# Block-sparse attention and an MLP mixer on one Trainium2 core: queries and keys loaded two tokens to a partition

## Chip, cores and metric

The kernel runs on one core of a Trainium2 chip. The metric is the device time of one execution in microseconds (us); less is better. Engines are called PE (TensorE), DVE (VectorE), ACT (ScalarE), POOL (GpSimd) and SP (SyncE), as in the profile. PEld is PE's loading of stationary operands.

## What is computed

Inputs are q, k and v of shape (4, 8, 768, 64) and four weight matrices, all float32. Each of the 32 heads does block-sparse causal attention: the keys form 12 blocks of 64, each query scores the mean key of each block up to its own, and it attends to the three best blocks and to its own.

```python
k_rep = k.reshape(B, H, n_blocks, block, D).mean(axis=3)
gate_scores = np.einsum('bhsd,bhnd->bhsn', q, k_rep)
causal = pos[:, None] // block >= np.arange(n_blocks)[None, :]
gate_scores = np.where(causal, gate_scores, -1000000000.0)
top_idx = np.argsort(gate_scores, axis=-1)[..., -top_k:]
...
scores = scale * np.matmul(q, k.transpose(0, 1, 3, 2))
mask = mask & (pos[:, None] >= pos[None, :])
scores = np.where(mask, scores, -1000000000.0)
...
return np.matmul(attn, v).astype(np.float32)
```

The heads of a batch side by side make x (768 tokens, 512 channels), which goes through an MLP over tokens (768 to 256 to 768) with a residual sum u, and an MLP over channels (512 to 1536 to 512) with another:

```python
h = np.maximum(xt @ w_tok1, 0.0) @ w_tok2
u = x + h.transpose(0, 2, 1)
h2 = np.maximum(u @ w_ch1, 0.0) @ w_ch2
return (u + h2).astype(np.float32)
```

## The kernel before

The work is cut into 16 head pairs (two heads of one batch each). For a pair, `prepare` does this:

- `load_qk` (L312) loads k and then q into `kl` and `ql`, one token to a partition and six tokens to a row, with one DMA for each head (L319). Each piece that a DMA moves is one head's 64 values of a token, 256 bytes.
- `transposes` (L358) turns six 128x128 tiles on PE, in float32. Both heads' channels become the 128 partitions, the 768 tokens the columns. `evac_t` (L367) copies that from PSUM to `kt` or `qt` on ACT.
- `cast` (L376) on POOL writes each head's 64 rows as float16 into `KA` and `QA`, the operands of the score matmuls. Pair 0 is cast on ACT (L383).
- `ksum` (L388) sums the keys of each block on DVE, and `kcopy` (L396) puts the sums of both heads into `ks2` with two small reductions.
- The gate: `gate_q` (pair 0), `gate`, `gate_s`, `gate_r` (pairs 1 to 5) or `gate_t`, `gate_e`, `gate_b` (groups of two and of four pairs) multiply q with the block sums and bring the result to queries on partitions. Tokens 0 to 127 need no gate: they have at most two blocks. So five tiles of 128 queries remain (`GJ`).
- On DVE, `gm` (L465) adds the causal bias, `top` (L482) takes the eight largest of each 12 with one MAX8 per head and tile (L489, ten to a pair), `below` (L492) compares with the third, and `bias` (L503) makes 0 or -30000 of it.
- `mask` (L513) turns the result on PE into PSUM, float16, 24 rows to a pair. `put_mask` (L522) copies it on DVE to rows 64 to 87 of `QA`, once per head (L525). The same rows of `KA` hold an indicator of each key's block, so that the score matmul of 88 rows adds the mask by itself.

The pairs are prepared in the groups [0], [1], [2], [3], [4], [5], [6, 7], [8 to 11] and [12 to 15]. Gate and mask are made for a whole group, the mask copies of a group follow one another (two to a pair).

`attend` then makes, for each head, three groups of score matmuls (`scores`, L529), their exponentials on ACT (`expo`, L547), the causal product on the diagonal blocks on DVE (`diag`, L555, line L559), the product with v (`av`, L563, line L571, two heads one after the other in one PSUM bank) and the normalization on DVE (`recip`, `norm`, L579 and L590). Tiles of five pairs (`R`) stand in a ring: the casts of pair i wait for the scores of pair i - 5.

The mixer of a batch runs as soon as its four pairs are there, and its matmuls stand between those of later pairs: token mixing in L602 and L614 (batch 0: L633 and L647), the sums u in L622 and L656, the channel MLP in L683 (ch1), its relu on ACT (L693) and DVE (L695), L704 (ch2) and the last sum in L712. Three PSUM banks (`bank`) serve gate, mask and mixer; two double banks (`big`) serve transposes and scores. v comes with a cast on POOL's DMA queue (L326), the weights too (L732 to L737); q, k and the outputs are on SP's.

The order in which each engine gets its instructions is fixed when the program is built. `plan` (L157) is given every operation with its engine, its cost in ns, its dependencies, its priority and the buffers that it takes. It goes through them in time, by these costs, and lists them; the engines then execute in that order. Costs stand in `prepare` and `attend` (a mask copy 410, a pair's MAX8 720, a load `size=1750`). Where PE has nothing to do before 46 us by this list, matmuls on zeros (`dummy`, L719, line L721) are put in, 122 of them. `VAFTER` says after which cast each load of v is issued.

Of the kernel before, what the change touches and what calls it, by code (L numbers as in the profile page):

```python
# [39 lines left out]
def QACT(i):  # L40
# [3 lines left out]
VAFTER = [("kt", 1), ("kt", 2), ("qt", 2), ("qt", 3), ("qt", 3), ("qt", 4), ("qt", 6), ("qt", 8),  # L44
          ("qt", 11), ("qt", 12), ("qt", 13), ("qt", 14), ("kt", 15), ("qt", 15), ("qt", 15), ("qt", 15)]
DIRECT = (0,)
WSIZE = (2400, 4500)
GATE = {1: 400, 2: 1000, 3: 1000, 4: 1000}
# [174 lines left out]
def kernel(  # L223
# [23 lines left out]
    GJ = NJ - 1  # L247
# [25 lines left out]
    ks2 = [sp.tile([128, 32], FP, tag=f"ks{r}", name=f"ks{r}") for r in range(R)]  # L273
    bn16 = [sp.tile([128, GJ, 128], F16, tag=f"bn{y}", name=f"bn{y}") for y in range(NBN)]
# [4 lines left out]
    own4 = sp.tile([128, 4 * GJ, 2 * NB], FP, tag="own4", name="own4")  # L279
    gbias = sp.tile([128, GJ, 2 * NB], FP, tag="gbias", name="gbias")  # L280
    gown = sp.tile([128, 3 * GJ * NB], FP, tag="gown", name="gown")
    gone = gown[:, 0:GJ * NB].rearrange("p (j n) -> p j n", n=NB)
    own = gown[:, GJ * NB:].rearrange("p (j c) -> p j c", c=2 * NB)
# [5 lines left out]
    gt = sp.tile([128, S - 128], FP, tag="gt", name="gt")  # L289
# [22 lines left out]
    def load_qk(i, t32, src):  # L312
        b, h = pairs[i]

        def f():
            t = sb(t32, [128, NJ, 2 * D], FP, f"{t32}_{i}")
            T[t32, i] = t
            for g in range(2):
                nc.sync.dma_start(out=t[:, :, D * g:D * g + D], in_=src[b, h + g].rearrange("(j p) d -> p j d", p=128))  # L319
        return f  # L320
# [13 lines left out]
    def twice(t):  # L334
        return t.rearrange("p j (x n) -> p j x n", x=1).broadcast_to([128, GJ, 2, NB])

# [8 lines left out]

    def own_four():
        for c in range(4):
            nc.gpsimd.tensor_copy(out=own4[:, c:4 * GJ:4, :], in_=own)
        nc.gpsimd.tensor_copy(out=gbias.rearrange("p j (x n) -> p j x n", n=NB), in_=twice(gone))
# [8 lines left out]
    def transposes(t32, i):  # L358
        def f():
            p = ps("big", None, f"t{t32}")  # L360
            T["tr", t32, i] = p
            t = T[t32, i]
            for j in range(NJ):
                nc.tensor.transpose(out=p[:, 128 * j:128 * j + 128], in_=t[:, j, :], identity=ident32)  # L364
        return f
# [10 lines left out]
    def cast(dst, name, i, x):  # L376
        def f():
            lo = 64 * x
            to, src = dst[i % R][x][0:64, :], T[name, i][lo:lo + 64, :]
            nc.gpsimd.tensor_copy(out=to, in_=src)  # L380
        return f

    def cast_act(dst, name, i, x):  # L383
        def f():
            nc.scalar.copy(out=dst[i % R][x][0:64, :], in_=T[name, i][64 * x:64 * x + 64, :])
        return f

    def ksum(i):  # L388
        def f():
            kst = sp.tile([128, NB], FP, tag="kst", bufs=2, name=f"kst_{i}")  # L390
            T["kst", i] = kst
            kt = T["kt", i]
            nc.vector.tensor_reduce(out=kst, in_=kt.rearrange("p (n w) -> p n w", w=64), axis=AX.X, op=ALU.add)  # L393
        return f

    def kcopy(i):  # L396
        def f():
            kst = T["kst", i]
            r = i % R
            for lo, c in ((0, 0), (64, NB)):  # L400
                nc.vector.tensor_reduce(out=ks2[r][lo:lo + 64, c:c + NB],
                                        in_=kst[lo:lo + 64, :].rearrange("p (n o) -> p n o", o=1),
                                        axis=AX.X, op=ALU.add)
        return f

    def gate_q(i):
        def f():
            g = ps("bank", [128, 512], "gps")
            T["gps", i] = g[:, 0:2 * NB * GJ].rearrange("p (j s c) -> p j s c", s=1, c=2 * NB)
            for j in range(GJ):  # L410
                nc.tensor.matmul(out=T["gps", i][:, j, 0, :], lhsT=T["qt", i][:, 128 * j + 128:128 * j + 256],
                                 rhs=ks2[i % R][:, 0:2 * NB], start=True, stop=True)
        return f

    def gate(i):
        def f():
            g = ps("bank", [128, 512], "gps")
            T["gtp", i] = g
            T["gps", i] = g[:, 192:192 + 32 * GJ].rearrange("p (j s c) -> p j s c", s=1, c=32)[:, :, :, 0:2 * NB]
            for lo, at, n, step in ((256, 64, 128, 128), (192, 0, 64, 0)):  # L420
                for s in range(4):
                    nc.tensor.matmul(out=g[32 * s:32 * s + 32, at:at + n], lhsT=ks2[i % R],
                                     rhs=T["qt", i][:, lo + step * s:lo + step * s + n], start=True, stop=True,
                                     tile_position=(0, 32 * s))
        return f

    def gate_s(i):
        return lambda: nc.scalar.copy(out=g1[i % 2][:, 64:256], in_=T["gtp", i][:, 0:192])

    def gate_r(i):  # L430
        def f():
            g, t = T["gtp", i], g1[i % 2]
            nc.tensor.transpose(out=g[:, 192:224], in_=t[0:32, 0:128], identity=ident32[0:32, 0:32])
            nc.tensor.transpose(out=g[:, 224:352], in_=t[:, 128:256], identity=ident32)
        return f

    def gate_t(gi):
        def f():
            p = ps("big", None, "gtp")
            T["gtp", gi] = p  # L440
            for a, e in ((0, 512), (512, S - 192)):
                for s, i in enumerate(GROUPED[gi]):
                    nc.tensor.matmul(out=p[32 * s:32 * s + 32, a:e], lhsT=ks2[i % R],  # L443
                                     rhs=T["qt", i][:, 192 + a:192 + e], start=True, stop=True,
# [3 lines left out]
    def gate_e(gi):  # L448
        def f():
            n = 32 * len(GROUPED[gi])  # L450
            nc.scalar.copy(out=gt[0:n, 64:S - 128], in_=T["gtp", gi][0:n, 0:S - 192])
        return f

    def gate_b(gi):
        def f():
            n = 32 * len(GROUPED[gi])
            p = ps("big", None, "gbp")
            g = p[:, 0:128 * GJ].rearrange("p (j s c) -> p j s c", s=4, c=32)
            T["gps", GROUPED[gi][0]] = g[:, :, 0:len(GROUPED[gi]), 0:2 * NB]
            for j in range(GJ):  # L460
                nc.tensor.transpose(out=p[:, 128 * j:128 * j + n], in_=gt[0:n, 128 * j:128 * j + 128],
# [3 lines left out]
    def gm(gi):  # L465
        def f():
            i, n = GROUPED[gi][0], len(GROUPED[gi])
            a = sb("gm", [128, GJ, 4, 2 * NB], FP, f"gm_{gi}")
            T["lt", gi] = a
            t = a[:, :, 0:n, :]  # L470
            T["gm", gi] = t
            if n == 1:
                nc.vector.tensor_tensor(out=t[:, :, 0, :].rearrange("p j (x n) -> p j x n", n=NB),
                                        in0=T["gps", i][:, :, 0, :].rearrange("p j (x n) -> p j x n", n=NB),
                                        in1=twice(gone), op=ALU.add)
                return
            nc.vector.tensor_tensor(out=t, in0=T["gps", i],
                                    in1=gbias.rearrange("p j (s c) -> p j s c", s=1).broadcast_to([128, GJ, n, 2 * NB]),
                                    op=ALU.add)
        return f  # L480

    def top(gi, s):  # L482
        def f():
            if s == 0:
                T["m8", gi] = sb("m8", [128, GJ, 4, 2, 8], FP, f"m8_{gi}")
            t = T["m8", gi]
            for j in range(GJ):
                for x in range(2):
                    nc.vector.max(out=t[:, j, s, x, :], in_=T["gm", gi][:, j, s, NB * x:NB * x + NB])  # L489
        return f  # L490

    def below(gi):  # L492
        def f():
            n = len(GROUPED[gi])
            t = T["gm", gi]
            m = T["m8", gi][:, :, 0:n, :, 2:3]
            nc.vector.tensor_tensor(
                out=t.rearrange("p j s (x n) -> p j s x n", n=NB),
                in0=t.rearrange("p j s (x n) -> p j s x n", n=NB),
                in1=m.broadcast_to([128, GJ, n, 2, NB]), op=ALU.is_lt)  # L500
        return f

    def bias(gi):  # L503
        def f():
            n = len(GROUPED[gi])
            out = bn16[gi % NBN].rearrange("p j (s c) -> p (j s) c", c=32)[:, :, 0:2 * NB]
            lt = T["lt", gi].rearrange("p j s c -> p (j s) c")
            for c in (slice(None),) if n == 4 else [slice(t, 4 * GJ, 4) for t in range(n)]:
                nc.vector.scalar_tensor_tensor(out=out[:, c, :], in0=lt[:, c, :], scalar=MASKV,
                                               in1=own4 if n == 4 else own, op0=ALU.mult, op1=ALU.max)  # L510
        return f

    def mask(gi):  # L513
        def f():
            n = 32 * len(GROUPED[gi])
            p = ps("bank", [128, 128 * GJ], "bps", F16)
            T["bps", gi] = p
            for j in range(GJ):
                nc.tensor.transpose(out=p[0:n, 128 * j:128 * j + 128], in_=bn16[gi % NBN][:, j, 0:n], identity=ident16)  # L519
        return f  # L520

    def put_mask(gi, s, x):  # L522
        def f():
            i = GROUPED[gi][s]
            nc.vector.tensor_copy(out=QA[i % R][x][64:MK, 128:S], in_=T["bps", gi][32 * s:32 * s + 2 * NB, :])  # L525
# [214 lines left out]
    def prepare(i):  # L740
# [7 lines left out]
        def last_scores(x):  # L748
            return [O.get(("sc", old, x, g)) for g in range(3)]

        for t32, src, off in (("kl", k, 0), ("ql", q, 0.1)):
            bf = Buf(t32)
            O[t32, i] = op("SP", 950, 0, [], pre - 12 + off, load_qk(i, t32, src), [bf], size=1750)
# [266 lines left out]
```

## Time and profile before

| | |
|---|---|
| median of 3 runs | 264.14 us (263.42 to 265.6) |
| the profiled execution | 264.1 us, span 262.4 us |
| PE busy | 253.8 us (97% of the span), granted clock 1.0 |
| DVE busy | 158.1 us (60%) |
| ACT busy | 146.4 us (56%) |
| POOL busy | 79.8 us (30%) |
| loads of q and k | 64 of 192 KB, 5.3 and 5.4 us from issue to landing in the median |
| DMA packets under 512 bytes | 84,896 of 91,323 |

The page gives the busy time of each engine, then the span in 40 slices of 6.6 us with the busy share of each in tenths. A group of instructions is one row: line, engine, operation, written tile and read tiles, shapes, count, then the summed busy time in us with the mean duration of one in ns, and the idle time of the engine just before them with what ended it. In a timeline the idle time before an instruction stands in brackets behind it. Durations of instructions that follow one another overlap by some 30 to 40 ns, so "start to start" is a little less than a duration.

### The profile page before, as it was taken

The numbers are of one execution on the slowest core, as the hardware profiler recorded it, in microseconds if no ns is written. First come the engines' busy times: TensorE is split into PE (matmuls) and PEld (weight loads), VectorE is DVE, ScalarE is ACT, GpSimd is POOL, SyncE is SP. The second block draws the span as 40 slices with busy tenths as digits, with TensorE's granted clock in tenths as the row PEclk, the third lists the DMA queues.
The fourth block names the chain that finished last, engine by engine and source line by source line (L and its number), as shares of the span: only waits on it lengthen the run. The fifth ranks groups of instructions, "written<-read, shape, count | busy, mean of one in ns | idle before, by whom it ended". The sixth has DMA issues, their size and how long they took to land.

```text
span 262.4 us, 5901 instructions
## 1 busy us (share of the span) xinstructions
PE 253.8 (97%) x2330; PEld 162.8 (62%) x2330; DVE 158.1 (60%) x539; ACT 146.4 (56%) x200; POOL 79.8 (30%) x112
## 2 busy tenths in 40 slices
PE   7999899999999999899999999999999999999994
PEld 7977588885776685566655766544455544466443
DVE  4569869998966499886598566462243253333222
ACT  3886998877899669677617999410034400044000
POOL 8299628974557462640730000000000000000000
PEclk9999999999999999999999999999999999999999
DMA  8999999999999974493193000008220035300032
GB/s 166 224 171 204 203 185 192 184 197 190 204 183 170 209 151 30 32 142 91 10 169 106 2 2 0 2 0 200 80 82 0 0 65 138 130 30 2 0 146 95
DMA packets 91323, 28.78 MB, mean 110 GB/s; under 512 B 84896, under 2 KB 87840, under 8 KB 91296
## 3 DMA queue, kind: packets, MB, share of 16 engines
q1 hardware_dynamic: 63232, 21.33, 38.5%
q0 software_dynamic: 28064, 7.08, 27.6%
q8 instruction: 18, 0.29, 0.5%
q14 instruction: 9, 0.07, 0.1%
HBM read 26.83 MB, written 6.29 MB: 126 GB/s over the span
## 4 chain that ended last, share of the span: by engine, by line
PE 74%; DVE 15%; DMA 5%; ACT 2%; issue 2%; POOL 1%; DVEq 0%; ACTq 0%
PE c L704 21%; PE c L683 20%; PE sps L539 10%; PE avp L571 6%; DMA V<-in_v_dram 5%; DVE QA L525 3%; DVE m L489 3%; PE avp L721 3%; PE ups L614 3%; PE tql L364 2%; PE tok L602 2%; PE tkl L364 2%; ACT e L552 1%; PE gtp L443 1%; DVE e L559 1%
## 5 line engine op out<-in xcount | busy, mean ns | idle before, releaser
L552 ACT ACTIVATE e<-sps 128x1024 f16<-128x1024 f32 (+1 forms) x96 | 84.0, 919 | 19.0 <-PE sps L539 18.1
L683 PE MATMUL c<-uT,wc 128*128 128x256 f16 (+1 forms) x384 | 69.9, 326 | 0.9 <-DVE QA L525 0.7
L704 PE MATMUL c<-wc,h 128*128 128x512 f16 (+2 forms) x300 | 64.8, 370 | 0.0
L693 ACT ACTIVATE h<-c 128x512 f16<-128x512 f32 x48 | 28.7, 598 | 58.0 <-PE c L683 57.7
L683 PEld LDWEIGHTS <-wc 128*128 128x128 f16 x384 | 36.5, 97 | 24.6 <-issue 1.1
L539 PE MATMUL sps<-QA,KA 88*128 88x512 f16 (+3 forms) x256 | 50.8, 306 | 0.9 <-ACT e L552 0.8
L704 PEld LDWEIGHTS <-h 128*128 128x128 f16 x300 | 28.8, 98 | 31.3 <-issue 0.6
L380 POOL CAST KA<-kt 64x768 f16<-64x768 f32 x30 | 25.1, 837 | 41.4 <-ACT kt L373 30.8
L712 DVE TENSOR_TENSOR ob<-u,c 128x512 f32<-128x512 f16 (+2 forms) x25 | 16.6, 666 | 34.8 <-PE c L704 34.7
L695 DVE TENSOR_SCALAR h<-c 128x256 f16<-128x256 f32 x48 | 20.3, 424 | 27.8 <-PE c L683 27.7
L559 DVE TENSOR_TENSOR e<-e,m 128x256 f16<-128x256 f16 x90 | 29.2, 333 | 13.1 <-ACT e L552 12.5
L539 PEld LDWEIGHTS <-KA 88*128 88x128 f16 x256 | 22.6, 98 | 17.1 <-issue 1.5
L380 POOL CAST QA<-qt 64x768 f16<-64x768 f32 x30 | 25.3, 842 | 11.5 <-ACT qt L373 10.1
L571 PE MATMUL avp<-V,e 128*128 128x65 f16 x672 | 26.7, 193 | 1.3 <-DVE e L559 0.9
L571 PEld LDWEIGHTS <-e 128*128 128x128 f16 x672 | 25.4, 97 | 3.8 <-DVE e L559 1.1
L373 ACT COPY kt<-tkl 128x768 f32<-128x768 f32 x16 | 12.8, 798 | 10.5 <-PE tkl L364 6.8
L393 DVE TENSOR_REDUCE kst<-kt 128x12 f32<-128x768 f32 x16 | 15.0, 945 | 6.0 <-ACT kt L373 5.9
L590 DVE TENSOR_TENSOR x<-avp,rc 128x384 f16<-128x384 f32 x32 | 17.8, 555 | 0.6
L326 POOL DMA_DIRECT2D V<-in_v_dram x16 | 16.4, 1030 | 0.0
L525 DVE COPY QA<-bps 24x640 f16<-24x640 f16 x32 | 14.2, 480 | 1.1 <-PE bps L519 0.8
L373 ACT COPY qt<-tql 128x768 f32<-128x768 f32 x16 | 12.8, 801 | 2.6 <-PE tql L364 2.4
L622 DVE TENSOR_TENSOR u<-x,ups 128x512 f16<-128x512 f16 x18 | 11.6, 683 | 3.9 <-PE ups L614 3.8
(75 smaller groups left out, 212.9 us busy)
## 6 DMA issues: line engine op xcount, KB each, us to landing
kl<-in_k_dram SPq DMA_DIRECT2D x32, 192.0 KB, 5.3
ql<-in_q_dram SPq DMA_DIRECT2D x32, 192.0 KB, 5.4
out_dram<-ob SPq DMA_DIRECT2D x23, 256.0 KB, 2.0
V<-in_v_dram POOLq DMA_DIRECT2D x16, 192.0 KB, 6.3
wc<-in_moe_w_ch_dram POOLq DMA_DIRECT2D x8, 384.0 KB, 8.4
w<-in_moe_w_tok_dram POOLq DMA_DIRECT2D x2, 384.0 KB, 8.4
out_dram<-ob SPq DMA_DIRECT2D x1, 160.0 KB, 1.8
out_dram<-ob SPq DMA_DIRECT2D x1, 96.0 KB, 1.7
```

The lines of the kernel that those rows point to most:

```text
L373: nc.scalar.copy(out=t, in_=p[:, 0:S])
L380: nc.gpsimd.tensor_copy(out=to, in_=src)
L525: nc.vector.tensor_copy(out=QA[i % R][x][64:MK, 128:S], in_=T["bps", gi][32 * s:32 * s + 2 * NB, :])
L539: nc.tensor.matmul(out=p[:, off + a:off + a + n], lhsT=KA[i % R][x][0:MK, 128 * kk:128 * kk + 128], rhs=QA[i % R][x][0:MK, q0 + a:q0 + a + ...
L552: nc.scalar.activation(out=e[:, 0:width], in_=T["sps", i, x, g][:, 0:width], func=AF.Exp, scale=scale)
L559: nc.vector.tensor_tensor(out=d, in0=d, in1=m0.rearrange("p (a b) -> p a b", a=1).broadcast_to([128, 2, 128]), op=ALU.mult)
L571: nc.tensor.matmul(out=p[:, jq, :], lhsT=T["e", i, x, g][:, o:o + 128], rhs=V16[i % (R + 1)][:, x, kk, :], start=(kk == 0), stop=(kk == jq))
L590: nc.vector.tensor_tensor(out=T["x16", b][:, :, 64 * hh:64 * hh + 64], in0=T["aps", i, x][:, :, 0:64], in1=T["rc", i, x].broadcast_to([128 ...
L683: nc.tensor.matmul(out=p, lhsT=wc1_16[:, cc, 128 * fc:128 * fc + 128], rhs=T["uT", b][:, cc, a // 128:e // 128, :], start=(cc == 0), stop= ...
L693: nc.scalar.activation(out=T["h2", b][:, fc, a:e], in_=T["c1", b, fc, n], func=AF.Relu)
L695: nc.vector.tensor_scalar(out=T["h2", b][:, fc, a:e], in0=T["c1", b, fc, n], scalar1=0.0, scalar2=None, op0=ALU.max)
L704: nc.tensor.matmul(out=T["c2", b, j, lo], lhsT=T["h2", b][:, fc, 128 * j:128 * j + 128], rhs=wc2_16[:, fc, lo:hi], start=(fc == 0), stop=( ...
```

## The change

q and k of a pair come in one DMA in place of two. A partition now takes two adjacent tokens of one head (512 bytes), and the six columns of tiles are three of head 0 and three of head 1. After the transposes, rows 0 to 63 of `kt` and `qt` are the channels of the even tokens and rows 64 to 127 those of the odd ones; the columns are head 0's 384 token pairs and head 1's.

The casts put the tokens back in order: one cast writes the even tokens of both heads to every second element of `KA` or `QA`, another the odd ones. Scores of either head now wait for all four casts, and the casts for the scores of both heads of pair i - 5.

The block sums come as halves, even and odd, and `kcopy` first brings the two halves together (two more reductions, with the other half's partitions as input), then adds them into `ks2`, which has a plane for each head. All six tiles of queries go through gate and mask now (`NM`), so there are twelve MAX8 to a pair in place of ten, six mask transposes for five, and the rows of 128 columns that were set to zero once are gone. The causal constants are laid out for token pairs; `own_four` on POOL and its operation in the list are gone, and `gm` and `bias` are one instruction per pair in the larger groups. `put_mask` writes with a step of two elements.

Costs in the list, `VAFTER` and `GATE` are changed too, and so is the order that `plan` makes of them.

```diff
-VAFTER = [("kt", 1), ("kt", 2), ("qt", 2), ("qt", 3), ("qt", 3), ("qt", 4), ("qt", 6), ("qt", 8),
-          ("qt", 11), ("qt", 12), ("qt", 13), ("qt", 14), ("kt", 15), ("qt", 15), ("qt", 15), ("qt", 15)]
+VAFTER = [("kt", 1), ("kt", 2), ("qt", 2), ("qt", 3), ("qt", 3), ("kt", 4), ("qt", 5), ("qt", 6),
+          ("qt", 10), ("qt", 11), ("qt", 13), ("qt", 14), ("kt", 15), ("qt", 15), ("qt", 15), ("qt", 15)]
-GATE = {1: 400, 2: 1000, 3: 1000, 4: 1000}
+GATE = {1: 340, 2: 1000, 3: 1000, 4: 1000}
...
-            for g in range(2):
-                nc.sync.dma_start(out=t[:, :, D * g:D * g + D], in_=src[b, h + g].rearrange("(j p) d -> p j d", p=128))
+            nc.sync.dma_start(out=t, in_=src[b, h:h + 2].rearrange("g (c p t) d -> p (g c) (t d)", p=128, t=2))
...
-            lo = 64 * x
-            to, src = dst[i % R][x][0:64, :], T[name, i][lo:lo + 64, :]
-            nc.gpsimd.tensor_copy(out=to, in_=src)
+    def spread(dst, i, t):
+        return dst[:, i % R].rearrange("p x s -> p (x s)")[0:64].rearrange("p (w t) -> p w t", t=2)[:, :, t]
+
+    def cast(dst, name, i, t):
+        return lambda: nc.gpsimd.tensor_copy(out=spread(dst, i, t), in_=T[name, i][64 * t:64 * t + 64, 0:S])
...
-            nc.vector.tensor_reduce(out=kst, in_=kt.rearrange("p (n w) -> p n w", w=64), axis=AX.X, op=ALU.add)
+            nc.vector.tensor_reduce(out=kst[:, :, 0], in_=T["kt", i].rearrange("p (n w) -> p n w", w=32), axis=AX.X, op=ALU.add)
...
+            for lo in (0, 64):
+                nc.vector.tensor_reduce(out=kst[lo:lo + 64, :, 1], in_=kst[64 - lo:128 - lo, :, 0:1], axis=AX.X, op=ALU.add)
             for lo, c in ((0, 0), (64, NB)):
-                nc.vector.tensor_reduce(out=ks2[r][lo:lo + 64, c:c + NB],
-                                        in_=kst[lo:lo + 64, :].rearrange("p (n o) -> p n o", o=1),
+                nc.vector.tensor_reduce(out=ks2[i % R][lo:lo + 64, :, c:c + NB],
+                                        in_=kst[lo:lo + 64].rearrange("p (g n) o -> p g n o", g=2),
                                         axis=AX.X, op=ALU.add)
...
-            for j in range(GJ):
-                for x in range(2):
-                    nc.vector.max(out=t[:, j, s, x, :], in_=T["gm", gi][:, j, s, NB * x:NB * x + NB])
+            for r in range(2 * NM):
+                nc.vector.max(out=T["m8", gi][:, s, r, :], in_=T["gm", gi][:, s, NB * r:NB * r + NB])
...
-            p = ps("bank", [128, 128 * GJ], "bps", F16)
+            p = ps("bank", [128, S], "bps", F16)
             T["bps", gi] = p
-            for j in range(GJ):
-                nc.tensor.transpose(out=p[0:n, 128 * j:128 * j + 128], in_=bn16[gi % NBN][:, j, 0:n], identity=ident16)
+            for m in range(NM):
+                t, c = m // (NM // 2), m % (NM // 2)
+                nc.tensor.transpose(out=p[0:n, 256 * c + 128 * t:256 * c + 128 * t + 128], in_=bn16[gi % NBN][:, m, 0:n], identity=ident16)
...
-            nc.vector.tensor_copy(out=QA[i % R][x][64:MK, 128:S], in_=T["bps", gi][32 * s:32 * s + 2 * NB, :])
+            nc.vector.tensor_copy(out=QA[i % R][x][64:MK, :].rearrange("q (c p t) -> q c t p", p=128, t=2),
+                                  in_=T["bps", gi][32 * s:32 * s + NG, :].rearrange("q (c t p) -> q c t p", p=128, t=2))
...
-        def last_scores(x):
-            return [O.get(("sc", old, x, g)) for g in range(3)]
+        last_scores = [O.get(("sc", old, x, g)) for x in range(2) for g in range(3)]
...
-            O[t32, i] = op("SP", 950, 0, [], pre - 12 + off, load_qk(i, t32, src), [bf], size=1750)
+            O[t32, i] = op("SP", 700, 0, [], pre - 12 + off, load_qk(i, t32, src), [bf], size=1300)
...
-                O["kcopy", i] = dve(200, [O["ksum", i], O.get(("gate", old))], pre + 1, kcopy(i))
+                O["kcopy", i] = dve(380, [O["ksum", i], O.get(("gate", old))], pre + 1, kcopy(i))
...
-            tops = [dve(720, [O["gm", gi]], pre + 3, top(gi, s)) if s == 0 else None for s in range(n)]
+            tops = [dve(860, [O["gm", gi]], pre + 3, top(gi, s)) if s == 0 else None for s in range(n)]
...
-                    O["put", m, x] = dve(410, [O["mask", gi]] + [O.get(("sc", m - R, x, g)) for g in range(3)],
+                    O["put", m, x] = dve(480, [O["mask", gi]] + [O.get(("sc", m - R, x, g)) for g in range(3)],
...
-                O["sc", i, x, g] = pe(occ, [O["put", i, x], O["cast", "kt", i, x], O["cast", "qt", i, x]] + ([ind_op[i]] if 0 < i < R else []), pr,
+                O["sc", i, x, g] = pe(occ, [O["put", i, x]] + [O["cast", n, i, t] for n in ("kt", "qt") for t in range(2)] + ([ind_op[i]] if 0 < i < R else []), pr,
```

## Prediction, written before the change was run

> **What bounds the kernel now.** I read the page first (busy times and the forty slices), then the chain, then the groups with shapes kept apart, then the timeline of PE and DVE and a table of DVE by stretch.
>
> ```profile
> PE 253.8 (97%) x2330; PEld 162.8 (62%) x2330; DVE 158.1 (60%) x539; ACT 146.4 (56%) x200; POOL 79.8 (30%) x112
> PE   7999899999999999899999999999999999999994
> DVE  4569869998966499886598566462243253333222
> DMA  8999999999999974493193000008220035300032
> ```
>
> PE is the bound over the whole. Its 122 warm-up matmuls (L721, 54 ns start to start, up to 28 us) are idle time in disguise, about 9 us; everything else is work. So only two things move the end: PE work added or removed, and PE standing still. DMA is full for the first 15 slices (98 us), DVE is nearly full in several slices before slice 22. Where PE stands still late in the run, the timeline of PE names DVE, with one DMA wait:
>
> ```profile
> 85.07 0.82 PE L571 MATMUL avp<-V,e 128*128 128x65 f16 x21 [0.39 <-DMA V<-in_v_dram]
> 102.96 0.60 PE L683 MATMUL c<-uT,wc 128*128 128x256 f16 x4 [0.29 <-DVE QA L525]
> 106.66 0.68 PE L571 MATMUL avp<-V,e 128*128 128x65 f16 x16 [0.94 <-DVE e L559]
> 141.59 0.60 PE L683 MATMUL c<-uT,wc 128*128 128x256 f16 x4 [0.42 <-DVE QA L525]
> ```
>
> The stops at 102.96 and 141.59 come at the end of eight mask copies (put_mask, L525) that DVE runs in one piece after each group of four head pairs. The chain shows the first piece, two copies to a row:
>
> ```profile
> 99.31 0.88 DVE QA L525 x2
> 100.20 0.89 DVE QA L525 x2
> 101.10 0.89 DVE QA L525 x2
> 102.00 0.91 DVE QA L525 x2
> ```
>
> DVE by stretch (start:end, length, busy, instructions):
>
> ```profile
> 46.00:60.00 14.00, 13.54 (x45) 1.00 1.24 189
> 60.00:74.00 14.00, 12.09 (x53) 1.00 1.23 196
> 89.60:110.00 20.40, 18.70 (x76) 1.00 0.69 85
> 130.50:144.60 14.10, 12.82 (x63) 1.00 1.12 132
> ```
>
> Idle DVE time there is 0.5, 1.9, 1.7 and 1.3 us. Between these stretches it is 6.6 us (74 to 89.6) and 6.7 us (110 to 130.5), after them 8.5 us (to 166). The change adds DVE work mostly to the full stretches.
>
> [...] 768 f16 elements from PSUM took 547 ns (L672), where f32 sources in PSUM cost about 1.05 ns an element (L712 below: 687 ns for 512, and its 320-element form 486). No row of before has a step of two. [...] the trace has only 256-byte pieces for q and k. [...]
>
> ```profile
> L525 DVE COPY QA<-bps 24x640 f16<-24x640 f16 x32 | 14.2, 480 | 1.1 <-PE bps L519 0.8
> L672 DVE COPY uT<-utps 128x768 f16<-128x768 f16 x4 | 2.2, 547 | 0.0
> L712 DVE TENSOR_TENSOR ob<-u,c 128x512 f32<-128x512 f16 x23 | 15.8, 687 | 34.1 <-PE c L704 34.0
> L489 DVE MAX8 m<-gm 128x8 f32<-128x12 f32 x160 | 12.8, 167 | 0.3
> L401 DVE TENSOR_REDUCE ks<-kst 64x12 f32<-64x12 f32 x32 | 4.9, 155 | 0.4
> L380 POOL CAST KA<-kt 64x768 f16<-64x768 f32 x30 | 25.1, 837 | 41.4 <-ACT kt L373 30.8 <-PE sps L539 9.6
> ```
>
> **The change, part by part.**
>
> *Loads.* A 256-byte packet takes 18 ns on its DMA engine, a 768-byte one of the same queue 36 and a 2048-byte one 85; the line through the last two puts 512 bytes at 26 ns. A load of q or k is 96 packets of 18 ns per engine now (1.73 us) and 48 of 26 ns then (1.25 us): 0.48 us less each, 15 us of transfer time over 32 loads. Almost all is hidden, since PE was busy. Uncovered are the first loads (packets of k0 end at 3.58, q0 at 5.34, q2 at 12.7 us; each is some 0.5, 1 and 3 us earlier) and the 0.39 us at 85. Bounds: no faster at all (0) to all of it early. SP issues 32 DMAs less, 0.5 us each; nothing waits for SP.
>
> *Mask copies.* The destination is now written with a step of two elements (24x3x2x128). [...] the price is L712's, 687 + 256 x 1.05 = 955 ns, 0.92 start to start, against 0.45 now. Lower bound, if the step costs nothing: L672's 547 ns, 0.52 start to start. I take 0.92[...]: +0.47 x 32 = 15.0 us of DVE. The kernel's list of costs, from which the order is made, counts 480 ns, so 0.44 us of each is not in the order.
>
> *Block sums (kcopy).* Two more small reductions, and a wait between the two pairs: 0.33 becomes about 0.70, x16 = +5.9 us. Behind the wait on DVE stand the gm and max of the pair, for which PE's scores wait in turn.
>
> *Top-3 (max).* Twelve in place of ten, 73 ns start to start: +0.15 x 16 = 2.4 us.
>
> *gm, below, bias.* 144 columns for 120 (+0.025 each); for groups of two and four gm and bias become one instruction per pair, about 0.27 each: four cost 1.1 where one cost 0.66 to 0.9. Together +2.5 us.
>
> DVE sum: 25.8 us. By stretch, from what the timeline holds in each: 9.8 to 26.4 six copies, three kcopies and three pairs' max and gm, 2.8 + 1.1 + 0.7 = 4.6; to 37.2 1.2; to 46 0.6; 46 to 60 four copies, three kcopies, one pair's max, 1.9 + 1.1 + 0.2 = 3.2; 60 to 74 four copies, two kcopies, two pairs', 1.9 + 0.7 + 0.6 = 3.2; to 89.6 0.7; 89.6 to 110 eight copies, two kcopies, four pairs', 3.8 + 0.7 + 1.5 = 6.0; to 130.5 0.7; 130.5 to 144.6 3.8 + 1.5 = 5.3. Less the idle time, the stretches run over by 1.5 (to 26.4, idle 3.1), 2.7, 1.3, 4.3 and 4.0 us.
>
> *PE.* Mask transposes +9 x 55 ns = 0.5; gate_b +3 x 109 ns = 0.3; gate_q +2 passes x 110 ns, covered by early idle. PE +0.8 us, some 0.6 uncovered after 46 us.
>
> *POOL.* own_four (1.3 us at 42) goes; nobody waited. The casts write with a step of 4 bytes; I price them unchanged at 0.84[...]. All four casts of a pair now precede its scores, in place of two: hidden, as the casts of pair 1 end at 16.7 and its mask copies at 22. A cast also waits for all six scores of the pair five before, in place of three; POOL waits 9.6 us for scores now (longest 4.4), all after 100 us, and behind it stand only V loads for pairs far ahead. Hidden too; without that cover the longest of these waits, 4 us, would be paid once.
>
> *ACT.* Evacuations and casts keep their sizes. Cost nothing.
>
> **Where the added DVE time becomes a PE stop.**
>
> - To 46 us: the loads release pair 1's gate (15.07 now, after q2's transposes) about 3 us sooner, but the new order puts three block sums, now dearer, ahead of its mask, so its first copy ends near 22.5 for 21.6 now. Both near-cancel: PE +0.2.
> - 46 to 60: 2.7 over. PE has token-mixing work that needs no DVE for part of it: +1.5.
> - 60 to 74: four copies stand in a row before the diagonal product that PE's next av needs, 1.3 over: +0.9.
> - 89.6 to 110: six copies in a row, then an add, a relu, a copy, an add, a copy. PE has transposes, one ch1 step, two ups steps and half a score, some 3 us, against 5.5 us of copies: +2.7.
> - 130.5 to 144.6: the order is copy, relu, four copies, relu, three copies, relu. The relus free PE's three banks and the diagonals behind them free av: 8 x 0.44 = 3.5 us of unplanned copy, nearly all seen: +3.3.
> - PE work +0.6; DMA wait at 85 gone, -0.4.
>
> Sum +8.8 us. The profiled execution took 264.1 us (span 262.4), the median of the shown runs is 264.14, so the sum applies unchanged: 272.9, I say 273.
>
> **Rivals.**
>
> 1. *The step costs nothing.* Copies at 0.52, close to what the order was made for. Then DVE grows by 13 us, all in the order, and the loads show: the new order has 97 warm-up matmuls for 122, 25 x 54 ns = 1.35 us less idle, the 0.4 us at 85 goes, PE work gives 0.6 back: 263; with one DVE overrun avoided 261.5. For it: nothing in before has the step. [...] It decides at a copy below about 0.6 us. Chance 0.14.
> 2. *Slow copies, but hidden.* The free 6.6, 6.7 and 8.5 us behind the full stretches take the overrun, and PE does other matmuls meanwhile: only two stops of about 1 us, +0.6 work: 266.5. Against: PE executes in its written order, and already stops at 102.96 and 141.59. Chance 0.18.
> 3. *POOL's casts slow too.* [...] POOL runs without a gap from 12 to 27 us with some 12 casts, so pair 2 and the V and weight loads come up to 5 us later: 278. For it: the writes are scattered. [...] Chance 0.10.
>
> My own case: 0.58.
>
> **How the numbers follow.** Own range: half of the stops, 268, to every overrun (1.5 + 2.7 + 1.3 + 4.3 + 4.0 + 0.6 = 14.4), 278.5. The range of 8 in 10 takes in rival 2 and the upper end of rival 3, and leaves out most of rival 1: 264 to 279. A measurement of this kernel tells about 1% (its runs spread 263.4 to 265.6), that is 261.5 and 266.8. Faster: a part of rival 1, 0.07. Same: the rest of it and half of rival 2, 0.17. Slower: 0.76.
>
> **What would show it.** The copy's row near 955 ns (547: rival 1). DVE over 90% busy from 89 to 110 and 130 to 148, and PE rows after the group masks with stops of 2 to 4 us in total behind copies or diagonals. Span of the PE rows from 165 on unchanged but shifted. q and k packets of 512 bytes near 26 ns, and the DMA slices thinner. Cast rows at 0.84. What would make it wrong: PE stops before 46 us of over 2 us either way, or filler that covers the copies.

## The result and the profile after

The changed kernel took 288.63 us in the median (287.95 to 289.33, 4 runs), the kernel before on the same chip 264.03: a ratio of 1.0922 (95%: 1.0862 to 1.0982), 24.6 us more. The forecast was 273, at most 279. The profiled execution took 289.33 us, its span is 287.6, so 25.2 us more than the span of before. (Of the four runs of the kernel with plain casts, below, two took over 1.5% more than the fastest, at a lower granted clock, and are left out of its ratio; its profile is one of them and is read for single durations alone.)

The page of the kernel after, the rows that were read of before:

```profile
PE 264.2 (92%) x2319; PEld 167.0 (58%) x2319; DVE 187.1 (65%) x615; ACT 148.1 (51%) x200; POOL 91.5 (32%) x107
PE   8987899898698999589999986999999999999995
DVE  3599969998987479997865998459224343143231
PEclk9999889999988899979999998999999999999999
DMA  7999999989976074009659700000712007210023
```

PE's share fell from 97 to 92%, with thin slices at the 11th, the 17th and the 25th. DVE did 29 us more, where 26 were forecast. And the row PEclk (the clock granted to PE, in tenths of full speed) has dips; before, it was full to the end:

```profile
PEclk9999999999999999999999999999999999999999
```

The groups of the kernel after (busy us, mean ns of one) show what became dearer. The last two rows together are `kcopy`:

```profile
L368 POOL CAST KA<-kt 64x768 f16<-64x768 f32 x30 | 31.8, 1059 | 62.2 <-ACT kt L361 36.8 <-PE sps L515 23.5 <-ACT e L528 0.8
L500 DVE COPY QA<-bps 24x768 f16<-24x768 f16 x32 | 30.9, 1005 | 1.9 <-PE bps L494 1.4
L386 DVE TENSOR_REDUCE ks<-kst 64x24 f32<-64x48 f32 x32 | 6.3, 197 | 0.9
L384 DVE TENSOR_REDUCE kst<-kst 64x24 f32<-64x24 f32 x32 | 5.5, 173 | 1.0
```

The copy (480 ns before) is a little over its forecast of 955, the cast (837 before) is not at the forecast 0.84 us. PE's own waits in the kernel after, by the line that it stood at and what it stood for:

```profile
PE avp L547 <- DVE e L535: 4.1, 4, 2.2
PE ups L590 <- DVE u L598: 3.7, 1, 3.7
PE sps L515 <- DVE gm L458: 2.4, 1, 2.4
PE gps L410 <- DVE ks L386: 2.0, 3, 0.9
PE bps L494 <- DVE bn L482: 1.8, 3, 1.1
```

The gaps between all PE rows, from the first matmul to the last, add up to 18.6 us; before it was 3.9. This is what is called standing below. The longest stop, in PE's timeline:

```profile
118.75 0.60 PE L659 MATMUL c<-uT,wc 128*128 128x256 f16 x4
123.03 1.01 PE L590 MATMUL ups<-h,w 128*128 128x512 f16 x2 [3.67 <-DVE u L598]
```

DVE's timeline of the same place names the cause: the add that frees PE stands behind six mask copies.

```profile
116.53 5.73 DVE L500 COPY QA<-bps 24x768 f16<-24x768 f16 x6
122.29 0.69 DVE L598 TENSOR_TENSOR u<-x,ups 128x512 f16<-128x512 f16 x1
```

There is a second loss, which no wait shows. The two matmuls at 123.03 take 1.01 us, where two such take 0.59 elsewhere (at 126.98). The table by stretch, cut at the edges of the clock's record, has PE's busy time first and the granted clock after POOL's:

```profile
119.32:122.73 3.41, 0.04 (x1) 0.00 (x0) 3.37 (x5) 0.66 (x1) 0.00 (x0) 1.00 0.00 0
122.73:126.15 3.42, 3.12 (x9) 1.27 (x9) 3.31 (x5) 1.02 (x1) 0.00 (x0) 0.50 0.00 0
126.15:129.56 3.41, 3.41 (x19) 1.60 (x17) 3.34 (x9) 1.27 (x2) 0.00 (x0) 1.00 0.00 0
```

After a stretch in which PE stood, PE ran at half clock for 3.41 us. The kernel after has five such stretches, from 33.99, 78.36, 92.01, 122.73 and 177.35 us, the kernel before none. At half speed each costs about 3.41 / 2 = 1.7 us, together 8.5. So, by this estimate, the 25.2 us divide into 14.7 us more standing and 8.5 us of half clock; a later start of the full clock (6.68 for 4.96 us, some 0.9), 0.8 of more PE work and 25 warm-up matmuls less (-1.35) nearly cancel; 1.6 us have no name.

### The profile page after: what moved, and what is told of

It is laid out like the page before. It is cut to its first block, busy times and chain, and to the rows that moved or that the text cites. A ratio compares the mean times of both kernels' runs of the same rounds, so it can differ in the third digit from the quotient of the medians.

```text
span 287.6 us, 5910 instructions
## 1 busy us (share of the span) xinstructions
PE 264.2 (92%) x2319; PEld 167.0 (58%) x2319; DVE 187.1 (65%) x615; ACT 148.1 (51%) x200; POOL 91.5 (32%) x107
## 4 chain that ended last, share of the span: by engine, by line
PE 68%; DVE 24%; issue 1%; ACT 1%; POOL 1%; DVEq 0%; POOLq 0%
PE c L680 21%; PE c L659 19%; PE sps L515 10%; DVE QA L500 9%; PE avp L547 6%; PE ups L590 3%; DVE kst L377 3%; DVE m L468 2%; PE tok L578 2%; PE tkl L352 2%; DVE ks L386 1%; PE tql L352 1%; DVE e L535 1%; DVE kst L384 1%; DVE h L671 1%
## 5 line engine op out<-in xcount | busy, mean ns | idle before, releaser
L659 PE MATMUL c<-uT,wc 128*128 128x256 f16 (+1 forms) x384 | 71.9, 337 | 1.2 <-DVE h L671 0.6
L515 PE MATMUL sps<-QA,KA 88*128 88x512 f16 (+3 forms) x256 | 52.7, 320 | 4.1 <-DVE gm L458 2.4
L659 PEld LDWEIGHTS <-wc 128*128 128x128 f16 x384 | 38.0, 101 | 26.0 <-issue 3.9
L368 POOL CAST KA<-kt 64x768 f16<-64x768 f32 x30 | 31.8, 1059 | 62.2 <-ACT kt L361 36.8
L535 DVE TENSOR_TENSOR e<-e,m 128x256 f16<-128x256 f16 x90 | 30.3, 357 | 8.9 <-ACT e L528 8.6
L368 POOL CAST QA<-qt 64x768 f16<-64x768 f32 x30 | 31.6, 1054 | 1.7
L500 DVE COPY QA<-bps 24x768 f16<-24x768 f16 x32 | 30.9, 1005 | 1.9 <-PE bps L494 1.4
L547 PE MATMUL avp<-V,e 128*128 128x65 f16 x672 | 28.3, 196 | 4.2 <-DVE e L535 4.1
L377 DVE TENSOR_REDUCE kst<-kt 128x24 f32<-128x768 f32 x16 | 15.1, 948 | 6.3 <-ACT kt L361 6.2
L468 DVE MAX8 m<-gm 128x8 f32<-128x12 f32 x192 | 15.1, 164 | 0.1
```

Source lines behind the costliest of these rows:

```text
L368: return lambda: nc.gpsimd.tensor_copy(out=spread(dst, i, t), in_=T[name, i][64 * t:64 * t + 64, 0:S])
L377: nc.vector.tensor_reduce(out=kst[:, :, 0], in_=T["kt", i].rearrange("p (n w) -> p n w", w=32), axis=AX.X, op=ALU.add)
L500: nc.vector.tensor_copy(out=QA[i % R][x][64:MK, :].rearrange("q (c p t) -> q c t p", p=128, t=2), in_=T["bps", gi][32 * s:32 * s + NG, :]. ...
L515: nc.tensor.matmul(out=p[:, off + a:off + a + n], lhsT=KA[i % R][x][0:MK, 128 * kk:128 * kk + 128], rhs=QA[i % R][x][0:MK, q0 + a:q0 + a + ...
L535: nc.vector.tensor_tensor(out=d, in0=d, in1=m0.rearrange("p (a b) -> p a b", a=1).broadcast_to([128, 2, 128]), op=ALU.mult)
L547: nc.tensor.matmul(out=p[:, jq, :], lhsT=T["e", i, x, g][:, o:o + 128], rhs=V16[i % (R + 1)][:, x, kk, :], start=(kk == 0), stop=(kk == jq))
```

## The experiments

Theory A: the slow mask copies fill DVE, PE stops behind it, and stops bring half-clock stretches. Rivals: the slower casts set the pace (B), or the block sums and the new order do (C). Each ratio is to the kernel before, run on the same chip; "us" is the median.

**Each addition taken out.**

In `put_mask`:

```diff
-out=QA[i % R][x][64:MK, :].rearrange("q (c p t) -> q c t p", p=128, t=2),
-in_=T["bps", gi][32 * s:32 * s + NG, :].rearrange("q (c t p) -> q c t p", p=128, t=2)
+out=QA[i % R][x][64:MK, :], in_=T["bps", gi][32 * s:32 * s + NG, :]
```

> The changed kernel, with the mask copies alone written without a step (the mask's columns stay in pair order, so tokens get the mask of another token of their block of 256). Theory A (the mask copies of 1005 ns fill DVE, PE stops behind it, and each stop of about 2 us is followed by 3.4 us at half clock): a copy falls to about 550 ns, DVE to about 172 us busy, at most two half-clock windows stay before the last one, and the time falls from 288.6 to 266 to 272. Theory B (POOL's casts, 1059 ns in place of 837, set the pace): the time stays above 283. Theory C (kcopy's extra reductions and the new order do it): above 280.

270.36 us, 1.0254 (1.0202 to 1.0307): 18.3 us of the 24.6 go. In its profile the copy took 548 ns, no half-clock stretch is left, and the gaps of PE fall from 18.6 to 8.2 us. A holds; B and C as sole causes fall.

In `spread`, which both casts use:

```diff
-return dst[:, i % R].rearrange("p x s -> p (x s)")[0:64].rearrange("p (w t) -> p w t", t=2)[:, :, t]
+return dst[:, i % R].rearrange("p x s -> p (x s)")[0:64, S * t:S * t + S]
```

> The changed kernel, with the casts alone written without a step (even and odd tokens of a pair of heads stay apart, so that the attention is over another order of tokens). A: a cast falls to about 840 ns, POOL to some 84 us busy, and the time stays within 3 us of 288.6, since the cast's end is seldom the last wait of a score. B: the time falls by 10 us or more, to below 279. C: no change.

1.067 (1.0622 to 1.0718), 281.5 us by the ratio: 7 us gained. This rests on two runs; the median of all four, 284.63 us, would make it 4. By either figure the casts are not hidden: A had put them at 3 us at most, B at 10 or more, C at nothing. The groups of this kernel show the cast's price:

```profile
L368 POOL CAST KA<-kt 64x768 f16<-64x768 f32 x30 | 24.8, 825 | 71.1 <-ACT kt L361 42.5 <-PE sps L515 27.6
```

Both edits together:

> The changed kernel, with mask copies and casts both written without a step (tokens not put back in order). A: as with the copies alone, 264 to 270, at most 2 us below it. B: 12 us or more below the run with the copies alone. C: still above 278.

267.68 us, 1.0156 (1.0121 to 1.0191), 2.7 us below the copies alone. The casts are worth more beside slow copies (7 us, or 4) than beside fast ones, which suggests that the two share stops; this isn't shown further.

In `kcopy`, on the changed kernel:

```diff
-for lo in (0, 64):
-    nc.vector.tensor_reduce(out=kst[lo:lo + 64, :, 1], in_=kst[64 - lo:128 - lo, :, 0:1], axis=AX.X, op=ALU.add)
...
-in_=kst[lo:lo + 64].rearrange("p (g n) o -> p g n o", g=2)
+in_=kst[lo:lo + 64, :, 0:1].rearrange("p (g n) o -> p g n o", g=2)
```

> The changed kernel without the two reductions that add the other parity's block sums (each block is then scored by half of its keys). DVE loses about 16 x 0.45 = 7 us of work, most of it in the full stretches. A: each us of DVE in a full stretch is worth up to one us of PE, and a half-clock window may go with it: 280 to 286. Rival (only the copies matter): 287 to 290.

282.37 us, 1.0713 (1.0668 to 1.0758): 6.3 us gained for 7 us of DVE. So the block sums count in their own right. Its profile's span is 8.0 us shorter, with 2.7 us less standing and three half-clock stretches fewer (5.1). The stop of 2.38 us that ends at 77.45 us shows where the standing was. First the kernel with plain copies, where it is as long as after, then this one:

```profile
71.48 0.61 PE L514 MATMUL sps<-QA,KA 88*128 88x512 f16 x3 [2.37 <-DVE gm L458]
```

```profile
73.73 0.61 PE L513 MATMUL sps<-QA,KA 88*128 88x512 f16 x3 [0.55 <-DVE gm L456]
```

Four block sums stand on DVE ahead of the gm that frees PE's buffer.

All three taken out at once (plain copies, plain casts, the short `kcopy`):

> The changed kernel with plain copies, plain casts and without the two extra reductions of the block sums (tokens not put back in order, each block scored by half of its keys): all three additions out, the loads, the order and the remaining small additions (12 maxima for 10, 144 columns for 120) in. A: the account closes, 262 to 265, as the kernel before. Rival (the new order itself costs something): 266 or more.

262.68 us, 0.9947 (0.9923 to 0.9971); PE's gaps are 2.1 us. The account closes: the loads, the order and the small additions together cost nothing beside the kernel before; they are 1 us faster.

**Each alone in the kernel before.** The copy's step:

```diff
-out=QA[i % R][x][64:MK, 128:S], in_=T["bps", gi][32 * s:32 * s + 2 * NB, :]
+out=QA[i % R][x][64:MK, 128:S].rearrange("q (c p t) -> q c t p", p=64, t=2),
+in_=T["bps", gi][32 * s:32 * s + 2 * NB, :].rearrange("q (c t p) -> q c t p", p=64, t=2)
```

> The kernel before, with the mask copies alone written with a step of two elements (the mask's columns are permuted within 128 tokens). Nothing else of the change is in it. A copy should take about 0.85 us in place of 0.48, 32 of them 12 us of DVE. A: stops of PE at the group masks of 102 and 141 us and in 46 to 74 us, one or two half-clock windows, time 270 to 278 against 264. C (the copies only hurt together with the other additions): 264 to 268.

275.55 us, 1.0436 (1.039 to 1.0481). The copy takes 863 ns for 480, so DVE does 32 x 0.383 = 12.3 us more, and the end moves by 11.7. So the copies cost time without the other additions, against C's 264 to 268. But not all of it is standing. The profiled execution's span is 10.0 us longer: PE's gaps grew by 7.4 us (11.3 for 3.9), one half-clock stretch (151.05) is 1.7, and 0.9 has no name. That is 0.6 us of standing for each us added to DVE.

The loads:

```diff
-for g in range(2):
-    nc.sync.dma_start(out=t[:, :, D * g:D * g + D], in_=src[b, h + g].rearrange("(j p) d -> p j d", p=128))
+nc.sync.dma_start(out=t, in_=src[b, h:h + 2].rearrange("g (c p t) d -> p (g c) (t d)", p=128, t=2))
```

> The kernel before, with the loads of q and k alone made as in the change: one DMA for a pair of heads, pieces of 512 bytes (so tokens come in another order; nothing puts them back). This is the gain that the change buys. The packets should take 28 ns for 512 bytes in place of 18 for 256, and the DMA slices get thinner. A (PE was covered): 262 to 264.5, under 1% below the kernel before. Rival (the loads hold the early stage back): 258 to 261, the start three us earlier.

263.71 us, 0.9997 (0.9981 to 1.0013): no gain. What the change buys was hidden already. Pair 1's gate matmuls started at 14.11 us in this kernel, 1 us sooner than before.

**The clock.** In the loop that emits the changed kernel's order:

```diff
+key = {id(o): n for n, o in O.items()}
+fill = {("sc", 5, 1, 0): 38, ("av", 6, 0): 20, ("umix", 1, 1): 60, ("av", 12, 0): 36}
 for o in order:
+    for n in range(fill.get(key.get(id(o)), 0)):
+        dummy(n)()
     o.fn()
```

> The changed kernel with 154 dummy matmuls of 54 ns (into an unused part of the accumulator's bank) in front of the four matmul groups that stand still longest: 38 ahead of the scores at 77 us, 20 ahead of the value product at 91, 60 ahead of the adds of token mixing at 123, 36 ahead of the value product at 176. They fill waits that stay as long as they are. A, with a clock term: the half-clock windows at 78, 92, 123 and 177 us go, and with them about 1.7 us each: 281 to 284 against 288.6, though PE does 8 us more work. Rival (the half-clock windows cost nothing beside the stops, or don't come from them): 288 or more, up to 290.

284.38 us, 1.0786 (1.076 to 1.0811): 4.2 us less for 8.3 us of added matmuls. PE's timeline at the longest stop now:

```profile
116.13 3.36 PE L697 MATMUL avp<-warm 128*128 128x122 f16 x60
120.00 0.59 PE L590 MATMUL ups<-h,w 128*128 128x512 f16 x2 [0.51 <-DVE u L598]
```

The two matmuls take 0.59 us again. Of the five half-clock stretches only the unfilled one (from 33.47) is left. The sum: gaps 6.7 us less, four stretches of 1.7 = 6.8 less, 8.3 of dummies more, so -5.2, against -4.2 in the medians and -4.7 between the two profiles. The half clock is a cost of its own and comes from PE standing.

**The order.** In the list of costs:

```diff
-O["put", m, x] = dve(480, [O["mask", gi]] ...
+O["put", m, x] = dve(940, [O["mask", gi]] ...
-O["kcopy", i] = dve(380, [O["ksum", i] ...
+O["kcopy", i] = dve(790, [O["ksum", i] ...
-occ = 770
+occ = 990
-O["gm", gi] = dve(240 * n, [gback] ...
+O["gm", gi] = dve(280 * n, [gback] ...
```

> The changed kernel with four costs in the list, from which the order of work is made, set to what the trace shows: mask copy 940 for 480, block sums 790 for 380, cast 990 for 770, gm 280 for 240 each pair. No instruction differs, only the order. The list's own end goes from 254.0 to 262.7 us. If most of the loss is that the order doesn't know the costs: 270 to 274, two half-clock windows at most. If the work itself has no cover (DVE full, whatever the order): above 280.

278.24 us, 1.056 (1.0537 to 1.0583): 10.4 us gained, between the two expectations. In its profile it has no half-clock stretch, and gaps of 12.9 us, none over 1.06. Knowing the costs, the order spreads the standing so thin that the clock stays; most of the standing itself remains. (5.8 us less standing and 8.5 of half clock would be 14.3; 1.5 of the difference are 28 more warm-up matmuls, the rest has no name.)

**The step moved elsewhere.** bias writes the values of a pair's two tokens side by side, and PE transposes them as one 4-byte word:

```diff
-bn16 = [sp.tile([128, NM, 128], F16, tag=f"bn{y}", name=f"bn{y}") for y in range(NBN)]
+bn16 = [sp.tile([128, NM // 2, 128, 2], F16, tag=f"bn{y}", name=f"bn{y}") for y in range(NBN)]
...
+for t in range(2):
+    half = slice(NM * NG // 2 * t, NM * NG // 2 * (t + 1))
+    nc.vector.scalar_tensor_tensor(out=bn16[gi % NBN][:, :, 32 * s:32 * s + NG, t],
...
+for c in range(NM // 2):
+    nc.tensor.transpose(out=p[0:n, 128 * c:128 * c + 128],
+                        in_=bn16[gi % NBN].rearrange("p c w t -> p (c w t)").bitcast(FP)[:, 128 * c:128 * c + n], identity=ident32)
```

> The changed kernel with the step moved from the mask copy to the bias: bias writes the mask values of the two tokens of a pair next to each other (two instructions per pair of heads in place of one, writing with a step of two), three transposes of 4-byte words take the place of six of 2-byte values, and the mask copies are then plain. Same list of costs, same order. The copies fall to about 550 ns (DVE -14.6 us), bias grows by some 16 x 0.15 = 2.4 us. A: as with the plain copies alone (270.4) plus up to 2: 270 to 273.

271.75 us, 1.0296 (1.0272 to 1.0321), as expected. It is the best form of the whole change that was found, and still slower than before.

With the measured costs in its list too:

> The last kernel with the measured costs in the list as well (mask copy 505, block sums 790, cast 990, gm 280), so that the order is made anew. The list's own end is 258.1 us, against 262.7 with the copies at 940 and 254.0 with the change's own list. A: 266 to 270, still not below the kernel before. Rival (the order is what was lost): 262 or below, since the loads then show.

272.14 us, 1.031 (1.0268 to 1.0353): no gain over the last, though the list's own end promised 258.1. Both expectations failed: with short copies, telling the list the measured costs gained nothing. Why the list's end is so far from the run's stays open.

Half of the copies, with the step, given to ACT (the other measured costs are in the list too):

```diff
-nc.vector.tensor_copy(out=QA[i % R][x][64:MK, :].rearrange("q (c p t) -> q c t p", p=128, t=2),
+(nc.scalar.copy if x else nc.vector.tensor_copy)(out=QA[i % R][x][64:MK, :].rearrange("q (c p t) -> q c t p", p=128, t=2),
...
-O["put", m, x] = dve(480, [O["mask", gi]] ...
+O["put", m, x] = (act if x else dve)(768 if x else 940, [O["mask", gi]] ...
```

> The changed kernel with the mask copies of every pair's second head on ACT (still with the step), the first head's on DVE, and the measured costs in the list (940, 768 columns on ACT, block sums 790, cast 990, gm 280). DVE loses 16 us, ACT gains some 12 and is then about 60% busy. The list's own end is 258.6. A (DVE's time is the bound, not the copies' latency): 267 to 273. Rival (a copy with a step is late on any engine, or ACT has no room): 276 or more, as with the measured costs alone (278.2).

290.29 us, 1.1 (1.0951 to 1.1049), far from A's 267 to 273 and in the rival's range. The timeline of ACT and DVE says why it doesn't decide between them:

```profile
114.21 1.01 DVE L500 COPY QA<-bps 24x768 f16<-24x768 f16 x1 [0.64 <-ACT QA L500]
115.25 1.00 ACT L500 COPY QA<-bps 24x768 f16<-24x768 f16 x1 [1.07 <-DVE QA L500]
```

The two engines take turns: each copy waits for the other engine's copy before it. So the eight copies take as long as on DVE alone, and ACT's other work stands behind them; for one such instruction (`h`, at 118.34) PE stood 3.75 us. The copies of a group read one tile of PSUM; whether that is why the built kernel has these waits wasn't tried. What ACT could do beside DVE stays open.

## Why the prediction was wrong

**Right.** PE as the bound, DVE as what stops it; the copy (955 forecast, 1005 measured), where I had only assumed that the step costs, since no row of before has one (without it the copy took 548 ns, and in the kernel before the step made 863 ns of 480); block sums at 0.80 for 0.70 us; the loads hidden (0.9997), with 512-byte packets at 28 ns for an estimated 26. Rival 1 fell with the copy's row. Rival 2 fell with the copy's step alone: 12.3 us of DVE moved the end by 11.7. Two readings were off, and nothing in the sum rests on them: the DMA row is full for 14 slices, not 15, and 122 x 54 ns is 6.6 us, not 9.

The table sets the forecast stops, in us, beside the standing that each stretch has more than before. The cuts follow the same work in each kernel: after, they are at 52, 69, 89, 92, 104, 130 and 160 us, with plain copies at 47.5, 63, 80, 85, 104, 115 and 150. Figures are rounded one by one.

| stretch of the kernel before | forecast | kernel after | with plain copies |
|---|---|---|---|
| to 46 us | 0.2 | 3.6 | 1.1 |
| 46 to 60 | 1.5 | 1.6 | 0.4 |
| 60 to 74, ahead of the gate's `gm` | none | 2.5 | 2.5 |
| 60 to 74, behind four copies | 0.9 | 1.3 | 0.5 |
| DMA wait at 85 | -0.4 | -0.4 | -0.4 |
| 89.6 to 110 | 2.7 | 2.6 | 0.2 |
| 110 to 130.5 | none | 0.4 | 0.4 |
| 130.5 to 144.6 | 3.3 | 2.9 | -0.4 |
| sum | 8.2 | 14.7 | 4.3 |

The four stops after 46 us that were forecast behind copies came as forecast, 8.5 us for 8.4, and nearly all of that goes with plain copies. That it fits so closely is in part luck: copies and block sums were dearer than in the estimate, and the casts held up DVE too. What failed lies elsewhere: of the 16 us beyond the forecast 8.5 are half clock, 3.4 standing before 46 us and 2.5 standing ahead of the `gm`.

**Failed: "PE +0.2" to 46 us.** The loads were to release pair 1's gate 3 us sooner than at 15.07, and its first copy to end near 22.5. With the new loads alone the gate came at 14.11; in the new order with all three additions out, at 15.51. In the kernel after it came at 17.48, as pair 1's block sums stood on DVE behind pair 0's slow copies:

```profile
14.63 1.93 DVE L500 COPY QA<-bps 24x768 f16<-24x768 f16 x2 [1.11 <-PE bps L494]
17.48 0.49 PE L410 MATMUL gps<-qt,ks 128*32 128x128 f32 x16 [0.81 <-DVE ks L386]
```

Pair 1's first copy began at 26.02. The mask transposes of pair 3 began at 29.22 us before and at 33.52 after, 4.3 us later and still ahead of the first half-clock stretch. With plain copies they came at 30.08, with plain casts as well at 29.19, with the short `kcopy` alone at 32.49. So taking out the copies gives 3.4 us of this delay back, the casts with them the rest, and the block sums alone 1.0; the shares overlap.

**Failed: block sums ahead of the `gm`.** The prediction names the wait ("behind the wait on DVE stand the gm and max of the pair"), but gave it no time of PE's. The stop of 2.38 us that ends at 77.45 us is this wait; without the extra reductions it is 0.55.

**Missing: the half clock.** No step had it, 8.5 us by the count of stretches, and it is the largest single miss. The trace of before shows none: it is at full clock from 4.96 us on, and after its first matmul PE stands for at most 0.94 us in one go (ahead of 106.66). In the kernel after, the half-clock stretches last 3.41 us each, and the full-clock stretches from the first to the last of them 40.96, 10.24, 27.31 and 51.20 us, which is 12, 3, 8 and 15 times that. So its record divides into windows of 3.41 us. Those with 2.38, 3.38 and 2.18 us of standing were followed by half clock, and two of the four with 1.16 to 1.38 us. In the 13 profiles other than that of the plain casts, between 20 and 255 us, every full-clock window with at least 1.86 us of standing was followed by half clock (11 of 11), of those with 1.1 to 1.74 us three of 22; what decides there stays open. A stop that straddles an edge is split: 2.38 us inside one window cost a stretch in the kernel after, 2.37 us across an edge (67.13 to 70.54 has 1.43 of standing, the next 0.95) none in the kernel with plain copies. So whether a stop costs a stretch depends on where the edges fall, and that differs from run to run: the first full-clock window starts between 4.03 and 7.29 us in these profiles.

**Failed: casts "unchanged at 0.84" and "hidden".** They took 1.06 us and were worth 7 us (4 by all four runs); rival 3 had the dearer cast, but in the early stage, and its price was my guess. A part goes by way of DVE. The trace of after shows it: DVE's causal product (L535) took 0.25 to 0.30 us when POOL was idle, and each of the 17 that started during a cast ended 0.08 to 0.14 us after that cast, taking up to 1.03 us. Here the last of three casts ends at 73.73 us and the product at 73.82:

```profile
70.49 3.25 POOL L368 CAST QA<-qt 64x768 f16<-64x768 f32 x3
72.81 1.01 DVE L535 TENSOR_TENSOR e<-e,m 128x256 f16<-128x256 f16 x1
```

The kernel before has this too (17 of 18 ended 0.14 to 0.19 us after the cast, and one took 0.93 us, at 51.90): 10 of its 90 products took over 0.35 us, 14 after. The same product ahead of the `gm` took 1.00 us with plain copies and 0.28 with plain casts as well, and the stop behind it fell from 2.37 to 1.74 us. How the rest of the casts' cost divides between this and late casts wasn't measured. ACT's casts of pair 0, put at no added cost, rose too, those of k from 830 to 1056 ns.

## What to carry to other kernels

Where an engine takes its work in a fixed order, as DVE does here (the add at 122.29 us came after 5.73 us of mask copies), and feeds the one that sets the end, follow its added time to each wait, small instructions and the first stage too: the two terms put at nearly nothing made 6 of the 6.5 us of standing beyond the forecast here. As a check on the sum, each us added to DVE became 0.5 us of PE standing in the whole change (14.7 of 29) and 0.6 with the copy's step alone (7.4 of 12.3). Then add a clock term, as measured here: count the windows of 3.41 us in which PE would stand for 1.86 us or more, at 1.7 us each. And a faster transfer that was already hidden bought nothing (0.9997 with the loads alone), while putting its data back in order is paid on the engines.

## What the runs showed of the hardware

- A step of two 2-byte elements in the written operand costs on each engine tried: DVE's copy from PSUM 548 to 1005 ns (24x768), POOL's cast 825 to 1059, ACT's cast 830 to 1056 (64x768 each). I had counted ACT's at nothing.
- PE ran at half clock for 3.41 us after each full-clock window of 3.41 us in which it stood for 1.86 us or more (11 of 11, between 20 and 255 us). 154 dummy matmuls in such stops shortened the run by 4.2 us.
- A two-input product on DVE (128x256, 0.25 to 0.30 us with POOL idle) that started during a POOL cast ended 0.08 to 0.14 us after it in the kernel after (17 of 17) and 0.14 to 0.19 us in the kernel before (17 of 18). In the kernel after, where it started 0.04 to 0.07 us ahead of a cast it took 0.28 or 0.29 us, and the cast 1.13 to 1.17 us in place of 1.03 to 1.07 (POOL's times are rough).
- A PE transpose of 4-byte words carried two f16 values side by side (mask values, 0 and -30000): three such, 274 ns each in the mean, in place of six of 221.
